# Pulling the conversion of a weight unit apart in the order of the work of a fused attention, gate and expert kernel

## The chip, the cores and the metric

The kernel runs on one core of a Trainium2 chip. The metric is the device time of one execution in microseconds (us), lower being better. Engines are called by the profile's names: PE is TensorE (PEld its weight loads), DVE is VectorE, ACT is ScalarE, POOL is GpSimd, and SP is SyncE, which here only issues transfers.

## The reference

Three stages follow one another, all in float32. The first is a gated linear recurrence over 768 steps for 4 x 8 heads of width 48, the second a gated feed-forward layer with 1536 hidden features, the third a choice of one of eight experts per token, each with 1024 hidden features.

```python
# stage 1, per batch and head
S_re, S_im = ar * S_re - ai * S_im + kv, ar * S_im + ai * S_re
y[:, :, t] = np.einsum('bhd,bhde->bhe', q[:, :, t], S_re)
...
# stage 2, 3072 tokens x 384; w_gate, w_val: 384 x 1536, w_out: 1536 x 384
xn = x / np.sqrt(np.mean(x * x, axis=-1, keepdims=True) + 1e-06) * rms_g
g = xn @ w_gate
x = (g / (1 + np.exp(-g)) * (xn @ w_val)) @ w_out
...
# stage 3
logits = xnorm @ en.T / tau          # en: 8 normalised expert embeddings
expert_idx = np.argmax(logits, axis=1)
out[mask] = gate_w[mask, None] * (np.maximum(x[mask] @ w1[e], 0.0) @ w2[e])
```

The three weights of stage 2 come in as float64, so each element has a low and a high 32-bit word.

## The kernel before, in words

The 3072 tokens are 24 tiles of 128. Stage 1 treats a tile in steps `s1` to `s10`; stage 2 treats blocks of two or three tiles (`BLOCKS`), and for each block runs over `NF` = 12 groups of 128 hidden features: `moe_g` (nine matmuls into `pg`, then a tanh on ACT and L799 on DVE), `moe_v` (nine matmuls into `pv`, L805, then the high part `hth` on ACT and the low part `htl` on DVE) and `moe_out` (three matmuls for each tile into `po`). While stage 2 works on one block, stage 1 prepares the tiles of the next.

Every float32 product is made of three matmuls with a high and a low part of each operand (`split_mm`). The parts of the weights are made once, during the first block, in 36 units: for each of the 12 groups one of w_gate, one of w_val, one of w_out. `conv_load(n)` lets SP load a unit (384 KB) into one of three `stg` buffers. `conv(n)` makes a float32 number out of the two words with three DVE instructions (L476 and L477 through the single buffer `ct`, L478 back into `raw`), copies it on ACT to the high part (L481), subtracts that on DVE for the low part (L482), and lets unit n + 3 be loaded.

For w_out there is also a fold. The router's logits come out of the same matmuls as the layer's output, in eight columns beside w_out's 384. For them PE turns the unit's `raw` by three transposes into a PSUM bank (`pwT`, L491), ACT copies it to SBUF (`wT`, L493), PE multiplies it by the embeddings in six passes (`pwe`, L496), and ACT and DVE make the two parts of the eight columns (L498, L499).

All steps are put on one list of events, each with a key in planned microseconds, and are written out in the order of the keys:

```python
for n in range(len(units)):
    at(CONV[0] + CONV[1] * n, conv, n)      # CONV = (-18.4, 1.85)
```

The first `moe_g` has key 0, and the first block has planned steps of 4.52 us for each group. Within what this order gives, the framework that compiles the kernel lays out each engine's instructions itself: of those that are ready by its own forecast, the one written first goes first. So the place of an instruction in the order is a priority, and the engines then work through their queues strictly in the order laid out.

Of the kernel before, what the change touches and what calls it, by code (L numbers as in the profile page):

```python
# [11 lines left out]
F32 = mybir.dt.float32  # L12
F32R = mybir.dt.float32r
I32 = mybir.dt.int32
AF = mybir.ActivationFunctionType
# [3 lines left out]
P = 128  # L19
# [14 lines left out]
T_BUFS = 3  # L34
# [66 lines left out]
SLOT = (0.0, 0.09, -0.43, 1.91, -1.0, -1.48, -0.61, -0.2, -0.3, -0.08, 0.0)  # L101
PACE = {0: 1.021, 2: 0.994}
CONV = (-18.4, 1.85)
ROUTE = 21.0
STARTUP = """
    s1.0 s1.1 s2.0 s2.1 s3a.0 s5a.0 s3a.1 s5a.1 s3b.0 s3b.1 s5b.0 s5b.1
# [185 lines left out]
def fused_kernel(ctx: ExitStack, tc: tile.TileContext, H, q, k, v, are, aim, wg, wv, wo, g, emb, tau, w1, w2, out):  # L292
    nc = tc.nc
    B, S, DM = q.shape
# [6 lines left out]
    NC = DM // P  # L301
# [30 lines left out]
    ident = beside[:, NC * E:]  # L332
# [31 lines left out]
    def bank(name):  # L364
        return psA.tile([P, 512], F32, tag="a", name=name)
# [90 lines left out]
    moe = wop.enter_context(tc.tile_pool(name="moe", bufs=1))  # L456
# [4 lines left out]
    units = [(src, dst, f) for f in range(NF) for src, dst in ((wg, WG), (wv, WV), (wo, WO))]  # L461
    raw_t = {}

    def conv_load(n):
        if n < len(units):
            src, _, f = units[n]
            raw_t[n] = moe.tile([P, DM, 2], I32, tag="stg", name="raw", bufs=STG_BUFS)
            nc.sync.dma_start(out=raw_t[n].rearrange("p x t -> p (x t)"), in_=src[f])

    def conv(n):  # L470

        _, dst, f = units[n]
        raw = raw_t.pop(n)
        lo, hi = raw[:, :, 0], raw[:, :, 1]
        t = moe.tile([P, DM], I32, tag="ct", name="ct", bufs=CT_BUFS)
        nc.vector.tensor_scalar(t, hi, 3, 0x3FFFFFF8, op0=ALU.logical_shift_left, op1=ALU.bitwise_and)  # L476
        nc.vector.scalar_tensor_tensor(out=t, in0=hi, scalar=-0x40000000, in1=t, op0=ALU.bitwise_and, op1=ALU.bitwise_or)  # L477
        nc.vector.scalar_tensor_tensor(out=hi, in0=lo, scalar=29, in1=t, op0=ALU.logical_shift_right, op1=ALU.bitwise_or)  # L478
        w = hi.bitcast(F32)
        dh, dl = (x[:, f, :DM] for x in dst)  # L480
        nc.scalar.activation(dh, w, AF.Copy)  # L481
        nc.vector.tensor_tensor(out=dl, in0=w, in1=dh.bitcast(F32), op=ALU.subtract)  # L482
        if dst is WO:
            fold(f, w)
        conv_load(n + 3)

    def fold(f, w):

        b = bank("pwT")
        for c in range(NC):  # L490
            nc.tensor.transpose(b[:, c * P:(c + 1) * P], w[:, c * P:(c + 1) * P], ident)  # L491
        wT = moe.tile([P, DM], F32, tag="t", name="wT", bufs=T_BUFS)
        nc.scalar.activation(wT, b[:, :DM], AF.Copy)  # L493
        pe = bank("pwe")[:, :E]
        for c in range(NC):
            nc.tensor.matmul(pe, wT[:, c * P:(c + 1) * P], enT[c], start=c == 0, stop=c == NC - 1)  # L496
        dh, dl = (x[:, f, DM:] for x in WO)
        nc.scalar.activation(dh, pe, AF.Copy)  # L498
        nc.vector.tensor_tensor(out=dl, in0=pe, in1=dh.bitcast(F32), op=ALU.subtract)  # L499
# [21 lines left out]
    st = {}  # L521
# [647 lines left out]
    def at(key, fn, *args):  # L1169
        events.append((key, len(events), fn, args))  # L1170
# [14 lines left out]
    for x, step in enumerate(STARTUP.split()):  # L1185
        fn, _, i = step.partition(".")
# [7 lines left out]
    at(-30.0, embed)  # L1194
    at(ROUTE, route_setup)
    start = 0.0
    prev = None
    for j, (t0, nt) in enumerate(blocks):
# [23 lines left out]
        if j:  # L1222
            jp, n = j - 1, blocks[j - 1][1]
# [8 lines left out]
            for x in range(per if j > 1 else 0):  # L1232
                n = (j - 2) * per + x
                at(start + (6.2 + 0.6 * x) * step, conv_load, n)
                at(start + (7.8 + 0.6 * x) * step, check_weight, n)
            for x in range(3 if j > 2 else 0):
                n = (j - 3) * 3 + x
# [3 lines left out]
        start += dur  # L1241
    for n in range(len(units)):
        at(CONV[0] + CONV[1] * n, conv, n)
    j = NB - 1
    t0, nt = blocks[j]
    begin = start - MOE_US * nt
# [85 lines left out]
```

## Time and profile before

| | |
|---|---|
| three runs | 1010.55, 1017.75, 1018.96 us; median 1017.75 us |
| profiled execution | 1016.29 us, of which the span of the trace 1014.5 us |
| busy share of the span | PE 94%, DVE 66%, ACT 60%, POOL 11% |
| mean granted clock of PE | 0.977 of full |

The span runs from the first to the last instruction; the remaining 1.8 us lie around it. A busy share is a mean over stages with different limits: the first block, in which the weights are converted, is only about an eighth of the span.

### The profile page before, as it was taken

Reading aid. Unit: us, or ns where it says so; the run is one execution under the profiler, and the core shown is the slowest. Engines: PE = TensorE matmul, PEld = TensorE weight load, DVE = VectorE, ACT = ScalarE, POOL = GpSimd, SP = SyncE. Lnnn points to the kernel's source line nnn. Section 1 sums busy time; section 2 is a strip of 40 time slices with the busy share of each in tenths; the row PEclk is TensorE's granted clock in tenths of the full one; section 3 lists DMA queues with packets and bytes.
Section 4 is the critical chain, followed back from the end, with each engine's and each line's share of the span. In section 5 each row is a group of like instructions: output and inputs, shape, how many; then the busy total and the mean of one; then the engine's idle time right before and its main releaser. Section 6 shows DMA issues by size and latency. Waiting matters only on the chain.

```text
span 1014.5 us, 19018 instructions
## 1 busy us (share of the span) xinstructions
PE 957.2 (94%) x7225; PEld 914.2 (90%) x7225; DVE 666.0 (66%) x1672; ACT 606.6 (60%) x1103; POOL 115.3 (11%) x174
## 2 busy tenths in 40 slices
PE   6968879999999999999999999999989999999995
PEld 5957778999999999999999999999988999999995
DVE  6887888777767867967976976654656544444420
ACT  7665757867678777767776855532434443455531
POOL 2000000100000100100010010010113211332211
PEclk9987789999999999999999999999999999999998
DMA  6353433215213412512511520300327423554200
GB/s 209 98 158 115 127 117 87 41 41 149 40 37 94 129 40 79 165 40 64 180 41 40 156 58 24 118 1 16 95 72 241 157 100 105 181 180 164 100 33 23
DMA packets 75539, 99.29 MB, mean 98 GB/s; under 512 B 27327, under 2 KB 57502, under 8 KB 75440
## 3 DMA queue, kind: packets, MB, share of 16 engines
q1 hardware_dynamic: 70272, 87.30, 28.9%
q0 software_dynamic: 5168, 10.70, 3.2%
q8 instruction: 58, 0.95, 0.4%
q14 instruction: 41, 0.34, 0.1%
HBM read 88.04 MB, written 10.50 MB: 97 GB/s over the span
## 4 chain that ended last, share of the span: by engine, by line
PE 73%; issue 8%; ACT 6%; DMA 5%; DVE 4%; POOL 1%; SPq 0%; POOLq 0%; ACTq 0%; DVEq 0%
PE pg L784 5%; PE po L784 4%; PE pg L785 4%; PE pg L786 4%; PE pv L784 4%; PE po L786 4%; PE pv L786 4%; PE pv L785 4%; PE po L785 4%; PE pAT L693 3%; PE ph L784 3%; PE ph L786 3%; PE ph L785 3%; PE eo L786 2%; PE eo L784 2%
## 5 line engine op out<-in xcount | busy, mean ns | idle before, releaser
L784 PE MATMUL pg<-xth,wg 128*128 128x384 f32 (+1 forms) x324 | 108.5, 335 | 7.8 <-DVE th L799 7.4
L436 ACT ACT_TABLE_LOAD x87 | 111.6, 1283 | 1.6
L784 PE MATMUL pv<-xth,wv 128*128 128x384 f32 (+1 forms) x324 | 106.7, 329 | 2.4 <-DVE th L805 2.4
L784 PE MATMUL po<-wo,hth 128*128 128x392 f32 x288 | 101.7, 353 | 3.6 <-ACT hth L807 3.6
L786 PE MATMUL pg<-xth,wg 128*128 128x384 f32 (+1 forms) x324 | 104.6, 323 | 0.0
L785 PE MATMUL pg<-xtl,wg 128*128 128x384 f32 (+1 forms) x324 | 104.5, 323 | 0.0
L786 PE MATMUL pv<-xth,wv 128*128 128x384 f32 (+1 forms) x324 | 104.4, 322 | 0.0
L785 PE MATMUL pv<-xtl,wv 128*128 128x384 f32 (+1 forms) x324 | 104.3, 322 | 0.0
L785 PE MATMUL po<-wo,hth 128*128 128x392 f32 x288 | 99.3, 345 | 0.0
L1083 DVE SCALAR_TENSOR_TENSOR hel<-ph,heh 128x256 fp32r<-128x256 f32 (+6 forms) x72 | 39.8, 553 | 89.9 <-ACT heh L1082 86.6
L786 PE MATMUL po<-wo,htl 128*128 128x392 f32 x288 | 98.5, 344 | 0.0
L436 ACT ACTIVATE th<-pg 128x384 f32<-128x384 f32 (+1 forms) x108 | 49.1, 455 | 80.1 <-PE pg L786 76.8
L807 ACT ACTIVATE hth<-th 128x384 fp32r<-128x384 f32 (+1 forms) x108 | 52.4, 485 | 67.2 <-DVE th L805 61.9
L1051 DVE TENSOR_TENSOR wl<-raw,wh 128x768 fp32r<-128x768 f32 x64 | 59.6, 955 | 33.7 <-ACT wh L1050 26.5
L1082 ACT ACTIVATE heh<-ph 128x256 fp32r<-128x256 f32 (+6 forms) x72 | 34.9, 485 | 75.4 <-PE ph L786 74.6
L799 DVE SCALAR_TENSOR_TENSOR th<-th,pg 128x384 f32<-128x384 f32 (+1 forms) x108 | 54.6, 506 | 33.7 <-ACT th L436 30.9
L784 PE MATMUL ph<-xeh,wh 128*128 128x256 f32 (+6 forms) x216 | 75.5, 350 | 0.0
L784 PEld LDWEIGHTS pg<-xth,wg 128*128 128x128 f32 x324 | 62.1, 192 | 12.8 <-DVE th L799 9.6
L786 PE MATMUL ph<-xeh,wl 128*128 128x256 f32 (+6 forms) x216 | 73.3, 339 | 0.0
L785 PE MATMUL ph<-xel,wh 128*128 128x256 f32 (+6 forms) x216 | 73.0, 338 | 0.0
L808 DVE TENSOR_TENSOR htl<-th,hth 128x384 fp32r<-128x384 f32 (+1 forms) x108 | 55.1, 511 | 22.3 <-ACT hth L807 20.7
L1050 ACT ACTIVATE wh<-raw 128x768 fp32r<-128x768 f32 x64 | 51.2, 839 | 29.6 <-DMA raw<-in_moe_w_dram 18.5
(250 smaller groups left out, 2500.5 us busy)
## 6 DMA issues: line engine op xcount, KB each, us to landing
raw<-in_moe_w_dram SPq DMA_DIRECT2D x32, 768.0 KB
raw<-in_moe_w_gate_dram SPq DMA_DIRECT2D x24, 384.0 KB
raw<-in_moe_w_val_dram SPq DMA_DIRECT2D x24, 384.0 KB
raw<-in_moe_w_out_dram SPq DMA_DIRECT2D x24, 384.0 KB
X<-in_a_im_dram SPq DMA_DIRECT2D x24, 192.0 KB
X<-in_a_re_dram SPq DMA_DIRECT2D x24, 192.0 KB
V<-in_v_dram SPq DMA_DIRECT2D x24, 192.0 KB
x2d<-row SPq DMA_DIRECT2D x24, 192.0 KB
```

The costliest lines, as they stand in the source:

```text
L436: chain[0] = fn(*args, **kw)
L693: nc.tensor.matmul(b[:, h * P:(h + 1) * P], KT[:D2, h], QT[:D2, h], start=True, stop=True)
L784: nc.tensor.matmul(o, lh, rh, start=start and x == 0, stop=False)
L785: nc.tensor.matmul(o, lh, rl, start=False, stop=False)
L786: nc.tensor.matmul(o, ll, rh, start=False, stop=stop and x == n - 1)
L799: nc.vector.scalar_tensor_tensor(out=t, in0=t, scalar=1.0, in1=b, op0=ALU.add, op1=ALU.mult)
L807: nc.scalar.activation(hh, t, AF.Copy)
L808: nc.vector.tensor_tensor(out=hl, in0=t, in1=hh.bitcast(F32), op=ALU.subtract)
L1050: nc.scalar.activation(dh, rw, AF.Copy)
L1051: nc.vector.tensor_tensor(out=dl, in0=rw, in1=dh.bitcast(F32), op=ALU.subtract)
L1082: nc.scalar.activation(hh, b, AF.Relu)
L1083: nc.vector.scalar_tensor_tensor(out=hl, in0=b, scalar=0.0, in1=hh.bitcast(F32), op0=ALU.max, op1=ALU.subtract)
```

## The change

The unit's work is spread over three events. `conv(n)` keeps the load's three DVE instructions and the copy to the high part. A new `split_weight(n)`, 1.2 units (2.22 planned us) later, makes the low part, for w_out also the transposes and the copy to `wT`, and lets unit n + 3 be loaded. `fold(f)`, 2.3 units (4.26 planned us) after the conversion, makes the eight columns. No instruction is added, removed or changed in size.

```diff
+SPLIT = (1.2, 2.3)
...
-        w = hi.bitcast(F32)
+        st["w", n] = hi.bitcast(F32)
+        nc.scalar.activation(dst[0][:, f, :DM], st["w", n], AF.Copy)
+
+    def split_weight(n):
+
+        _, dst, f = units[n]
+        w = st.pop(("w", n))
         dh, dl = (x[:, f, :DM] for x in dst)
-        nc.scalar.activation(dh, w, AF.Copy)
         nc.vector.tensor_tensor(out=dl, in0=w, in1=dh.bitcast(F32), op=ALU.subtract)
         if dst is WO:
-            fold(f, w)
+            b = bank("pwT")
+            for c in range(NC):
+                nc.tensor.transpose(b[:, c * P:(c + 1) * P], w[:, c * P:(c + 1) * P], ident)
+            st["wT", f] = moe.tile([P, DM], F32, tag="t", name="wT", bufs=T_BUFS)
+            nc.scalar.activation(st["wT", f], b[:, :DM], AF.Copy)
         conv_load(n + 3)
 
-    def fold(f, w):
-
-        b = bank("pwT")
-        for c in range(NC):
-            nc.tensor.transpose(b[:, c * P:(c + 1) * P], w[:, c * P:(c + 1) * P], ident)
-        wT = moe.tile([P, DM], F32, tag="t", name="wT", bufs=T_BUFS)
-        nc.scalar.activation(wT, b[:, :DM], AF.Copy)
+    def fold(f):
+
+        wT = st.pop(("wT", f))
         pe = bank("pwe")[:, :E]
...
     for n in range(len(units)):
         at(CONV[0] + CONV[1] * n, conv, n)
+        at(CONV[0] + CONV[1] * (n + SPLIT[0]), split_weight, n)
+        if n % 3 == 2:
+            at(CONV[0] + CONV[1] * (n + SPLIT[1]), fold, n // 3)
```

## Rows read from the trace of the kernel before

**Rows 1.** Busy time by stretch: its length, each engine's busy us, PE's clock, DMA.

```profile
46.00:166.00 120.00, 96.08 (x741) 87.04 (x741) 96.34 (x234) 73.36 (x143) 3.14 (x8) 0.86 0.40 119
...
200.00:1014.50 814.50, 791.95 (x5804) 763.54 (x5802) 503.72 (x1240) 471.94 (x850) 101.64 (x126) 0.99 0.31 93
```

**Rows 2.** DVE's waits, 46 to 180 us: us in total, times, longest.

```profile
DVE wo L499 <- ACT wo L498: 6.2, 8, 1.7
DVE wv L482 <- ACT wv L481: 3.3, 2, 2.3
DVE wg L482 <- ACT wg L481: 2.6, 2, 1.4
DVE ss L755 <- ACT XN L754: 2.3, 2, 1.9
...
DVE A L695 <- PE pAT L693: 1.4, 2, 0.9
DVE Sn L718 <- PE pKV L710: 0.6, 1, 0.6
```

**Rows 3.** PE's waits in the same stretch.

```profile
PE pwe L496 <- ACT wT L493: 6.2, 8, 2.0
PE pwT L491 <- issue: 5.8, 3, 2.7
```

**Rows 4.** ACT's longest group of waits in the same stretch.

```profile
ACT wo L481 <- DVE raw L478: 17.1, 7, 3.8
```

**Rows 5.** The transfer queue's longest group of waits, 0 to 180 us.

```profile
SPq L468 <- DVE wo L482: 23.1, 9, 4.2
```

**Rows 6.** Timeline of DVE around one unit of w_out, in order of time.

```profile
86.16 0.56 DVE L478 SCALAR_TENSOR_TENSOR raw<-raw,ct 128x384 int32<-128x384 int32 x1
...
87.63 0.55 DVE L482 TENSOR_TENSOR wo<-raw,wo 128x384 fp32r<-128x384 f32 x1
...
89.75 0.17 DVE L499 TENSOR_TENSOR wo<-pwe,wo 128x8 fp32r<-128x8 f32 x1 [1.01 <-ACT wo L498]
89.83 0.55 DVE L478 SCALAR_TENSOR_TENSOR raw<-raw,ct 128x384 int32<-128x384 int32 x1
...
96.51 0.15 DVE L755 TENSOR_SCALAR ss<-ss 128x1 f32<-128x1 f32 x1 [1.91 <-ACT XN L754]
```

**Rows 7.** Timeline of PE: the fold of that unit, and a later one.

```profile
86.82 0.60 PE L491 MATMUL pwT<-beside,raw 128*128 128x128 f32 x3 [1.83 <-issue]
88.06 1.45 PE L496 MATMUL pwe<-beside,wT 128*128 128x8 f32 x6 [0.64 <-ACT wT L493]
...
129.15 0.83 PE L496 MATMUL pwe<-beside,wT 128*128 128x8 f32 x6 [0.64 <-ACT wT L493]
```

**Rows 8.** Timeline of DVE: its four waits before a subtraction of wg or wv.

```profile
49.11 0.56 DVE L482 TENSOR_TENSOR wv<-raw,wv 128x384 fp32r<-128x384 f32 x1 [0.96 <-ACT wv L481]
...
78.88 0.56 DVE L482 TENSOR_TENSOR wg<-raw,wg 128x384 fp32r<-128x384 f32 x1 [1.41 <-ACT wg L481]
...
119.62 0.56 DVE L482 TENSOR_TENSOR wg<-raw,wg 128x384 fp32r<-128x384 f32 x1 [1.24 <-ACT wg L481]
...
151.18 0.56 DVE L482 TENSOR_TENSOR wv<-raw,wv 128x384 fp32r<-128x384 f32 x1 [2.33 <-ACT wv L481]
```

**Rows 9.** Groups that touch raw: shortest, median, longest ns; first and last start.

```profile
L476 DVE TENSOR_SCALAR ct<-raw x36: 338/353/450, 11.8 to 159.5; 128x384 int32<-128x384 int32 x36
...
L478 DVE SCALAR_TENSOR_TENSOR raw<-raw,ct x36: 536/553/560, 16.0 to 161.0; 128x384 int32<-128x384 int32 x36
...
L468 SPq DMA_DIRECT2D raw<-in_moe_w_gate_dram x12: 327/347/433, 6.0 to 146.4; - x12
...
L482 DVE TENSOR_TENSOR wg<-raw,wg x12: 528/550/560, 17.4 to 157.3; 128x384 fp32r<-128x384 f32 x12
```

**Rows 10.** Timelines of SP and DVE: the load with the shortest lead, and its use.

```profile
43.47 0.33 SPq L468 DMA_DIRECT2D raw<-in_moe_w_val_dram  x1
```

```profile
46.60 0.36 DVE L476 TENSOR_SCALAR ct<-raw 128x384 int32<-128x384 int32 x1 [0.21 <-DMA raw<-in_moe_w_val_dram]
```

## The prediction, made before the changed kernel was run

> **What bounds the kernel now.** I read the busy time by stretch first, because the mean over the span hides where this change lies. From 200 us on PE works 791.95 of 814.50 us at a clock of 0.99: that part is bound by PE, and nothing in it is touched. The first block, from 46 to 166 us, is another matter: PE is busy for 96.08 of 120 us at a clock of 0.86, DVE for 96.34, ACT for 73.36 [rows 1]. No engine is full there. DVE has the least to give: its work up to the end of the block is fixed, and PE's 96 us would shrink with a higher clock, while DVE's would not. So I take the block's end to be DVE's 96.34 us plus what DVE idles, 120 - 96.34 = 23.7 us. Later work on PE moves one for one with that end. The change can win at most 23.7 us, and only by taking DVE idle time away.
>
> Second, I read who waits for whom in that stretch. DVE waits longest before the last step of the fold, 6.2 us in 8 waits, and 3.3 + 2.6 = 5.9 us in four waits before the subtractions L482 of wv and wg; behind these come waits for stage 1 steps on PE and ACT, among them 2.3, 1.4 and 0.6 us [rows 2]. PE itself stands 6.2 us before the fold's six passes, because ACT has not yet copied `wT`, and 5.8 us before the transposes [rows 3]. That second wait is printed as "issue", but in the unit at 86 us the transposes start at 86.82, when L478 has just ended at 86.16 + 0.56 = 86.72 [rows 6, 7]: PE stands there for the converted numbers. ACT waits 17.1 us for the same L478 before copying w_out's high part [rows 4], and what stands behind that copy in its queue, a tanh among others, waits too.
>
> Third, the timeline of one fold. From L478's end at 86.72 to L499's start at 89.75 the chain over transposes, copy, six passes and L498 lasts 3.03 us, of which DVE idles the last 1.01 [rows 6, 7]. So the fold is a round trip through three engines, each of which works strictly in order.
>
> **The change part by part.** No instruction comes or goes, so all busy times stay; only places move. What moves is the priority in the order from which the engines' queues are laid out, so I price each part as if the instruction lands just behind the work that now outranks it.
>
> *Subtraction L482.* It now comes behind the next unit's three DVE instructions. Its four waits are 0.96, 1.41, 1.24 and 2.33 us [rows 8], together 5.94. A full-size DVE instruction of the conversion takes 0.55 us, the small L476 0.35 [rows 9]. At 78.88 two instructions of the next unit (L477, L478) still follow and can step in front: 1.1 us hidden. At 119.62 all three follow, 1.45 us: the whole 1.24 is hidden. At 151.18 only L478 follows: 0.55. At 49.11 the next unit isn't loaded yet: nothing. Sum 2.9 us gained; bounds 0 (the layout keeps its order) and 5.9.
>
> *Fold's end L499.* Its waits are 6.2 us. Of the 3.03 us chain, 88.06 - 86.72 = 1.34 us (transposes and copy) no longer stand directly ahead of the passes; the passes themselves, 0.83 us at the full clock and 1.45 at the lower one [rows 7], still stand directly ahead of L498 and L499. About half of the round trip leaves, so I take half: 3.1 us; bounds 0 and 6.2.
>
> *Transposes, copy and passes on PE and ACT.* PE's 12.0 us before them [rows 3] are not counted for themselves, as PE isn't the bound here. They count where DVE waits for what stands behind the fold in PE's queue: the longest of three groups, 1.9, 0.9 and 0.6 us [rows 2], follow a fold directly (the one at 96.51 goes back over PE to the fold at 88.06 [rows 6, 7]). Half of these 3.4 us is 1.7; bounds 0 and 3.4.
>
> *The load of unit n + 3.* This is the price. SP issues it once a buffer is free, and already waits 23.1 us, 9 times, for the L482 of a w_out unit [rows 5]. Nothing else on SP waits for it, save that the in-order queue can now put it behind a load of V or QK that itself waits. I set L482 of each unit behind the next unit's L478: over 35 pairs that is 2.6 us later on average (36 units, [rows 9]; in the unit at 87.63 it is 89.83 + 0.55 - 87.63 = 2.75 [rows 6]). Then I compare each of the 33 later loads with its use: the lead from issue to L476 runs from 3.13 to 10.4 us. At 3.13 DVE waited 0.21 us for the landing [rows 10], so 3.13 us is about what a load takes. Eleven loads would come late, by 14.0 us together. Three of them (units 6, 7 and 9, 10.8 us) lie between 36 and 54 us, where buffers are held by the first two transposes of w_out, and where a subtraction can't stay behind a unit that waits for its own buffer; I leave those out. The other eight make 3.2 us. Bounds 0 and 14.0.
>
> [...]
>
> *`wT` and the PSUM banks.* `wT` is held longer in a tag of three buffers, which it shares with `th`; one `th`, at times two, is alive, so I cost this at nothing. If two were always alive, a tanh would wait for the six passes, up to 1.45 us a time [rows 7].
>
> *Sum.* 2.9 + 3.1 + 1.7 - 3.2 = 4.5 us gained. The profiled execution took 1016.29 us (span 1014.5 and 1.8 around it), which gives 1011.8. It lies 1.46 us under the median of the three runs, so I forecast 1013. With all gains and no price it is 1017.75 - 15.5 = 1002; with the whole price and no gain 1032.
>
> **The rivals.** *The whole stretch tightens, PE's clock included: 1003.* [...] If the 12 us before the fold go and the clock comes back, transposes and scores of stage 1 reach DVE sooner, and the waits of rows 2 shrink by about 14 to 15 us. For it speaks that gaps precede the slow passages; against it, that PE's waits for `th` and `hth` come from DVE and stay. [...]
>
> *Nothing moves: 1017.* The order is only a priority: where an engine is free in the forecast of the layout, it takes the transposes as soon as they are ready, whatever their key. PE has room, so the fold may stay where it is.
>
> *Late loads bind: slower, 1029.* With a buffer held 2.6 us longer in each of 36 units, all eleven late loads hold up DVE: 14.0 us, less the 2.9 at L482, on 1017.75. It decides from the point where the lead of the loads after 50 us, mostly 5 to 6 us now, falls under 3.13. Against it: DVE lays out other work in front where the load isn't there.
>
> **How the numbers follow.** The forecast (1008 to 1017 for itself) has 0.47, the tight stretch 0.22, no movement 0.17, late loads 0.14. The three runs before spread over 8.4 us, so a change within 1% (10.2 us) can hardly be told from none. Faster by over 1%, under 1007.6: the tight stretch and the low edge of the forecast, 0.27. Slower by over 1%, above 1027.9: most of the late loads, 0.11. Within: 0.62. The range from 1002 to 1025 leaves out most of the late loads and a low tail, under 0.2 together.
>
> **What would show it.** In the profile after: L482 of a unit behind the next unit's L478 on DVE, its waits near 3 us; the passes `pwe` no longer waiting for `wT`; L499's waits near 3; the first block ending some 5 us sooner, and the work after it unchanged in length. I am wrong if L476 shows waits for loads of several us, if ACT's wait before w_out's copy grows, or if the first block ends early and the gain is given back later.

## The result: 1.3% faster, and the profile after

The changed kernel took 1000.78 us in the median of four runs (999.60 to 1003.51), the kernel before 1016.23 us in its four (1010.55 to 1018.96): a ratio of 0.9868, 95% interval 0.9826 to 0.9909. The interval lies wholly below 1: a small gain, but clear of the spread, and about three times what the forecast's sum gave. The profiled execution took 1003.51 us, with a span of 1001.8 us, 12.7 us less than before.

In the changed file L477 to L479 are the three instructions of the conversion, L488 is the subtraction, L492 the transposes, L494 the copy to `wT`, L502 the six passes, and L504 and L505 make the eight columns.

First, where in the span the time was won. These are the busy times by stretch of the kernel after, the two that answer to [rows 1] and then the stretch from 46 us to the start of the last subtraction (length, PE, PEld, DVE, ACT and POOL busy, PE's clock, DMA):

```profile
46.00:166.00 120.00, 103.17 (x865) 92.40 (x864) 106.16 (x276) 85.81 (x172) 4.13 (x11) 0.93 0.45 131
200.00:1001.80 801.80, 778.91 (x5697) 749.83 (x5687) 495.85 (x1225) 462.50 (x833) 102.13 (x125) 0.99 0.31 93
...
46.00:150.30 104.30, 87.65 (x748) 77.27 (x747) 92.47 (x230) 73.60 (x144) 3.26 (x9) 0.92 0.48 142
```

The stretch up to the last subtraction in the kernel before:

```profile
46.00:162.30 116.30, 92.96 (x681) 84.79 (x679) 94.18 (x230) 71.35 (x138) 3.14 (x8) 0.85 0.41 123
```

The last subtraction comes after 104.3 instead of 116.3 us. DVE does 230 instructions in both; its busy time goes from 94.2 to 92.5, its idle time from 22.1 to 11.8 us. So 10.3 of the 12.0 us are DVE idle time taken away, and PE's clock rises from 0.85 to 0.92. The same 12.0 us can be booked on PE: 5.3 us less busy time, though with 748 instead of 681 instructions, and 6.7 us less idle time. The split by DVE alone doesn't tell which engine carried the gain. The groups of the first stage 2 result rows, of before and after (x24: shortest, median, longest ns, then first and last start):

```profile
L828 ACT ACTIVATE row<-po x24: 473/492/508, 172.1 to 753.1; 128x384 f32<-128x384 f32 x24
```

```profile
L834 ACT ACTIVATE row<-po x24: 474/492/504, 157.3 to 739.5; 128x384 f32<-128x384 f32 x24
```

The first block ends 14.8 us sooner, and 13.6 of that is still there at the end of stage 2: what lies behind is bound by PE and only shifts.

Second, the waits. DVE's in the kernel after, 46 to 150.3 us (total, times, longest):

```profile
DVE wg L488 <- ACT wg L481: 4.1, 3, 3.3
DVE wo L505 <- ACT wo L504: 1.7, 1, 1.7
DVE ct L477 <- DMA raw<-in_moe_w_gate_dram: 1.3, 2, 0.7
DVE xtl L783 <- ACT xth L782: 1.2, 1, 1.2
DVE QK L631 <- ACT En L437: 1.2, 1, 1.2
DVE wv L488 <- ACT wv L481: 0.9, 1, 0.9
DVE htl L814 <- ACT hth L813: 0.8, 1, 0.8
DVE A L701 <- PE pAT L699: 0.4, 1, 0.4
DVE ct L477 <- DMA raw<-in_moe_w_val_dram: 0.3, 1, 0.3
DVE th L805 <- ACT th L437: 0.2, 1, 0.2
```

In the kernel before, 46 to 162.3 us, beside the lines of [rows 2] for wv, wg, A and Sn, which hold for this stretch too:

```profile
DVE wo L499 <- ACT wo L498: 5.5, 7, 1.7
DVE ss L755 <- ACT XN L754: 1.9, 1, 1.9
DVE xtl L777 <- ACT xth L776: 1.9, 2, 1.2
DVE R L635 <- ACT R L634: 1.7, 1, 1.7
DVE th L799 <- ACT th L436: 1.2, 2, 0.9
DVE htl L808 <- ACT hth L807: 1.1, 1, 1.1
```

I sort these lines by whose work is waited for. Before the subtraction: 5.9 us before, 5.0 after. Before the eight columns: 5.5, now 1.7. For a load: 0.2, now 1.6. For steps of stage 1 and of the hidden features (ss, xtl, R, A, th, htl, Sn, QK): 1.9 + 1.9 + 1.7 + 1.4 + 1.2 + 1.1 + 0.6 = 9.8, now 3.8. The last sort fell most, though none of these steps was touched.

Third, the same unit of w_out as in [rows 6, 7], in PE's timeline after:

```profile
83.65 0.52 PE L492 MATMUL pwT<-beside,raw 128*128 128x128 f32 x3
...
84.25 0.81 PE L607 MATMUL T<-X,triS 128*128 128x384 f32 x2
84.89 0.89 PE L607 MATMUL L<-X,triS 128*128 128x384 f32 x2
...
86.69 0.28 PE L792 MATMUL pv<-xth,wv 128*128 128x256 f32 x1
86.84 0.83 PE L502 MATMUL pwe<-beside,wT 128*128 128x8 f32 x6
```

and in DVE's:

```profile
81.65 0.55 DVE L479 SCALAR_TENSOR_TENSOR raw<-raw,ct 128x384 int32<-128x384 int32 x1
...
84.59 0.14 DVE L761 TENSOR_SCALAR ss<-ss 128x1 f32<-128x1 f32 x1
...
90.87 0.16 DVE L505 TENSOR_TENSOR wo<-pwe,wo 128x8 fp32r<-128x8 f32 x1
```

The transposes start 1.45 us after L479 has ended (82.20) and wait for nothing; the passes start 3.2 us after them, with other matmuls between, `T` and `L` of stage 1 among them; the passes run at the faster pace (0.83, not 1.45 us) amid `pv`; the columns' low part follows 3.2 us after their end without a wait. And `ss`, for which DVE stood 1.91 us in [rows 6], is there when DVE comes to it.

That wait for `ss` shows a second thing. PE makes `pKV` and eight groups `pyT` for it: before, right behind the fold of [rows 7]; after, ahead of the same unit's fold. First and last of them, before with the clock, then after:

```profile
89.44 1.50 PE L710 MATMUL pKV<-V,KF 128*32 128x48 f32 x48
...
93.91 0.54 PE L740 MATMUL pyT<-QT,Sn 96*64 96x128 f32 x4
```

```profile
88.00:92.00 4.00, 3.94 (x66) 3.80 (x68) 2.24 (x7) 2.80 (x7) 0.77 (x1) 0.50 0.35 103
```

```profile
79.61 0.88 PE L716 MATMUL pKV<-V,KF 128*32 128x48 f32 x48
...
82.01 0.39 PE L746 MATMUL pyT<-QT,Sn 96*64 96x128 f32 x4
```

Before, PE had stood 1.83 and 0.64 us at the fold [rows 7], its clock was then 0.50, and this work took 5.01 us; after, it takes 2.79 us at a clock of 1.00. The difference of 2.2 us is more than the 1.91 us that DVE waited. So this wait can be owed to the clock as much as to the place in the queue.

### The profile page after: what moved, and what is told of

Read it like the earlier page. It is cut to its first block, busy times and chain, and to the rows that moved or that the text cites. A ratio compares the mean times of both kernels' runs of the same rounds, so it can differ in the third digit from the quotient of the medians.

```text
span 1001.8 us, 19020 instructions
## 1 busy us (share of the span) xinstructions
PE 951.2 (95%) x7225; PEld 905.6 (90%) x7225; DVE 663.4 (66%) x1672; ACT 605.5 (60%) x1103; POOL 116.0 (12%) x174
## 4 chain that ended last, share of the span: by engine, by line
PE 69%; DVE 9%; issue 8%; DMA 6%; ACT 5%; POOL 1%; SPq 0%; POOLq 0%; ACTq 0%; DVEq 0%
PE pg L790 4%; PE pv L790 4%; PE po L790 4%; PE pg L791 4%; PE pg L792 4%; PE pv L791 4%; PE po L792 4%; PE pv L792 4%; PE po L791 4%; PE pAT L699 3%; PE ph L790 3%; PE ph L791 3%; PE ph L792 3%; PE eo L791 2%; PE eo L792 2%
## 5 line engine op out<-in xcount | busy, mean ns | idle before, releaser
L791 PE MATMUL pv<-xtl,wv 128*128 128x384 f32 (+1 forms) x324 | 104.3, 322 | 0.0
L1089 DVE SCALAR_TENSOR_TENSOR hel<-ph,heh 128x256 fp32r<-128x256 f32 (+6 forms) x72 | 39.9, 554 | 90.5 <-ACT heh L1088 87.7
```

What stands on the lines that cost most here:

```text
L791: nc.tensor.matmul(o, lh, rl, start=False, stop=False)
L1089: nc.vector.scalar_tensor_tensor(out=hl, in0=b, scalar=0.0, in1=hh.bitcast(F32), op0=ALU.max, op1=ALU.subtract)
```

## The experiments

Each ratio is to the kernel before, run beside it on the same chip; a 95% interval stands in brackets. Where nothing else is said, a shown line of busy times is the stretch from 46 us to the last subtraction's start. DVE's idle time is the length less its busy time. The lines come from one execution of each run, which need not be a typical one: that of sub_late (1014.09 us) and that of fill_low (1026.66) were the slowest of ten, that of half (1011.78) the slowest but one, and that of sub_early (998.90) the fastest of four.

**Only the eight columns late** (fold_late).

```diff
-        at(CONV[0] + CONV[1] * (n + SPLIT[0]), split_weight, n)
+        at(CONV[0] + CONV[1] * n, split_weight, n)
```

> Only the eight columns (six passes, L498, L499 of before) are put 2.3 units later; the low part, the transposes, the copy to wT and the load stay with the conversion. If the gain is the fold's round trip taken apart, this alone gives most of it: 1001 to 1006 us, no waits of PE for wT, and the columns' wait on DVE under 2.5 us. If the lower place of the subtraction and the transposes does it, this stays at 1012 to 1017. If any change of the order that closes PE's gaps helps through the clock, the time follows the clock of the first block: 0.92 and about 1002, or 0.86 and about 1016.

Ratio 0.9924 [0.9898, 0.9950], 1007.08 us. Busy times by stretch, and PE's longest waits in it:

```profile
46.00:153.20 107.20, 84.30 (x671) 77.06 (x670) 93.56 (x227) 70.49 (x138) 3.27 (x8) 0.90 0.45 133
```

```profile
PE pwT L492 <- issue: 5.5, 2, 3.7
PE pg L790 <- DVE th L805: 4.9, 2, 2.8
...
PE pwT L492 <- DVE raw L479: 3.0, 2, 2.1
```

Over half of the gain, a little short of what I expected. PE waits for `wT` only once more, for 0.6 us, but it waits longer for the converted numbers, 8.5 us before the transposes. DVE's idle time is down to 13.6 us all the same. The third theory fits too: between its two points (0.86 and 1016 us, 0.92 and 1002) the clock of 0.90 asks for about 1007 us.

**The fold late as a whole** (split_late).

```diff
-SPLIT = (1.2, 2.3)
+SPLIT = (1.2, 1.2)
```

> Low part, transposes, copy, load and the eight columns all come 1.2 units after the conversion, the eight columns straight behind the transposes. The fold is as closely knit as before, only later as a whole. Round trip theory: little gained, 1010 to 1016, PE still waits 4 us or more for wT. Theory that the lower priority of all this work is what counts (conversion and tanh go first): 1001 to 1006.

Ratio 0.9916 [0.9874, 0.9958], 1006.07 us:

```profile
46.00:153.20 107.20, 86.86 (x741) 76.67 (x739) 92.67 (x230) 73.85 (x144) 3.37 (x9) 0.92 0.47 137
```

My theory of the round trip missed here: a fold as closely knit as before, but 1.2 units later, gains as much as the columns alone, and DVE idles 14.5 us. Lower priority counts, not only the distance between the links; the clock is 0.92 here as well. DVE still waits 4.2 us before the columns in this run.

**Only the subtraction and the load late** (sub_late).

```diff
     def conv(n):
...
+        # transposes and copy to wT, as in split_weight
     def split_weight(n):
...
         nc.vector.tensor_tensor(out=dl, in0=w, in1=dh.bitcast(F32), op=ALU.subtract)
         conv_load(n + 3)
...
-            at(CONV[0] + CONV[1] * (n + SPLIT[1]), fold, n // 3)
+            at(CONV[0] + CONV[1] * n, fold, n // 3)
```

> Only the subtraction for the low part and the load come 1.2 units later; transposes, copy and eight columns stay with the conversion. The predicted 2.9 us at the subtraction less 3.2 us for late loads: 1016, within 3 us of before. If the subtraction's place were the cause of the gain: 1001 to 1008.

Ratio 0.9968 [0.9943, 0.9993], 1011.62 us:

```profile
46.00:161.20 115.20, 94.73 (x676) 85.10 (x675) 93.31 (x227) 71.49 (x139) 3.14 (x8) 0.82 0.41 124
```

A small gain, with DVE's idle time unchanged at 21.9 us in the execution shown. Its waits before the subtraction are 3.0 us there instead of 5.9, the 2.9 us that I had set, but waits at other lines (A 4.0, th 3.7) make up for them. In its timeline the subtraction stands behind the next unit's last conversion instruction in 6 of 35 units (1 before, 7 in the changed kernel): the lower priority hardly moves it. I take it that the layout found it ready before its rivals; no run shows that.

**All but the subtraction late** (sub_early).

```diff
     def conv(n):
...
+        nc.vector.tensor_tensor(out=dl, in0=w, in1=dh.bitcast(F32), op=ALU.subtract)
     def split_weight(n):
...
-        nc.vector.tensor_tensor(out=dl, in0=w, in1=dh.bitcast(F32), op=ALU.subtract)
```

> As the changed kernel, but the subtraction stays with the conversion; transposes, copy and load come 1.2 units later, the eight columns 2.3 units later. If the fold is the cause: as the changed kernel, 999 to 1004. If the subtraction carries 2.9 us of the gain: 1003 to 1006.

Ratio 0.9885 [0.9834, 0.9935], 1001.37 us, as the changed kernel (0.9868):

```profile
46.00:150.20 104.20, 85.74 (x745) 75.38 (x744) 92.93 (x228) 73.81 (x144) 3.43 (x9) 0.93 0.48 141
```

The subtraction's place adds nothing that can be seen; the intervals, half a per cent to either side, would hide its 2.9 us. The transposes, the copy, the load and the columns carry the gain, and since early_load below gains nothing by earlier loads, the fold's later place is the cause.

**Only the columns' two halves late, the passes in place** (cols_late). The passes' result goes to SBUF by an added copy.

```diff
+        st["pc", f] = sm.tile([P, E], F32, tag="pc", name="pc")
+        nc.scalar.activation(st["pc", f], pe, AF.Copy)
...
+        pc = st.pop(("pc", f))
-        nc.scalar.activation(dh, pe, AF.Copy)
-        nc.vector.tensor_tensor(out=dl, in0=pe, in1=dh.bitcast(F32), op=ALU.subtract)
+        nc.scalar.activation(dh, pc, AF.Copy)
+        nc.vector.tensor_tensor(out=dl, in0=pc, in1=dh.bitcast(F32), op=ALU.subtract)
```

> As the kernel before, but ACT first copies the six passes' result to a small SBUF tile (12 added copies of 128x8), and only the two halves of the eight columns (L498, L499 of before) are made 2.3 units later; the transposes, the copy to wT and the passes stay with the conversion. If DVE's own wait before L499 (5.5 us) is what the later fold saves: 1009 to 1011 us and no such wait. If the passes standing in PE's queue ahead of stage 1 work are the cause: no gain, 1013 to 1017.

Ratio 0.9983 [0.9959, 1.0007], 1012.17 us. Busy times, then DVE's longest waits:

```profile
46.00:159.80 113.80, 90.72 (x681) 81.55 (x679) 94.28 (x230) 72.84 (x149) 3.14 (x8) 0.87 0.43 126
```

```profile
DVE wg L488 <- ACT wg L481: 4.3, 4, 2.7
DVE A L707 <- PE pAT L705: 3.6, 3, 2.4
...
DVE wo L511 <- ACT wo L510: 2.6, 3, 1.7
```

DVE's wait before the columns falls from 5.5 to 2.6 us, and the time is the same within the interval: other waits (wg 4.3 for 2.6, A 3.6 for 1.4) take its place. What DVE waits for is late anyhow, as PE still does the passes early and ACT waits 4.6 us for them in the added copy (4.2 us before, at L498). The 12 copies are also 2.1 us of added work on ACT, so this run takes that one wait away and not the whole fold's end.

**PE kept busy** (filled: 48 groups of six 128x128 matmuls of `ones` and `ident` in planned order, float32; fill_low: 12 groups of 16 in float32r, the type of the split weights, of the lowest priority in the block).

```diff
+    def fill(n):
+        b = psO.tile([P, 512], F32, tag="o2", name="fill")
+        for _ in range(n):
+            nc.tensor.matmul(b[:, :P], ones, ident, start=True, stop=True)
...
+    for n in range(48):
+        at(0.3 + 1.1 * n, fill, 6)
```

```diff
+        w = WG[0][:, f, :P]
+        for _ in range(16):
+            nc.tensor.matmul(b[:, :P], w, w, start=True, stop=True)
...
+    for n in range(NF):
+        at(53.5, fill, n)
```

> The kernel before with 288 matmuls of 128x128 that nobody reads, written into a PSUM bank that is free in the first block, spread over that block. They keep PE busy without changing what waits for what. If the clock of PE is what the change gave back: clock of the first block from 0.85 to 0.95 and more, and 1001 to 1008 us. If the waits come from the order of the queues: clock up, time 1012 to 1022.

> The kernel before with 192 short matmuls that nobody reads (high-part weights, 128x128, about 0.06 us each), 16 for each feature group, of the lowest priority in the first block, into a free PSUM bank: about 12 us of PE work in gaps of 23 us, where the 576 longer ones of the run named filled had made PE full. If PE's clock is the cause of the gain: clock of the first block over 0.90 and 1005 to 1011 us. If the cause is what stands in the queues ahead of stage 1 work: clock up, time 1012 to 1019.

filled: ratio 1.0245 [1.0202, 1.0288], 1038.12 us. fill_low: 1.0028 [1.0000, 1.0056], 1020.87 us. Their stretches, and the group of the added instructions in the first (288 matmuls appear as 576):

```profile
46.00:153.30 107.30, 107.01 (x977) 102.19 (x976) 90.48 (x215) 63.72 (x124) 3.22 (x8) 1.00 0.45 134
```

```profile
L389 PE MATMUL fill<-beside,ones x576: 269/275/378, 50.3 to 191.7; 128*128 128x128 f32 x192
```

```profile
46.00:155.80 109.80, 100.99 (x805) 94.12 (x803) 94.35 (x229) 71.51 (x140) 3.15 (x8) 0.91 0.43 131
...
L835 ACT ACTIVATE row<-po x24: 473/492/505, 180.6 to 760.0; 128x384 f32<-128x384 f32 x24
```

The first made PE full and tells only that PE's time in this block isn't free. The second brings the clock from 0.85 to 0.91, near the 0.92 of the changed kernel, and the last subtraction comes 6.5 us sooner: DVE's idle time is 15.5 instead of 22.1 us, although 122 of the added matmuls take 18.5 us of PE there (0.15 us each, not the 0.06 that I had expected; a third of the 0.17 us from start to start of the 128x384 matmuls at 230 to 236 us of the kernel before would be 0.06). But the first block's rows come at 180.6, 8.5 us later than before. The other 70 added matmuls lie in between. From the last subtraction to the first row, of fill_low and of before:

```profile
155.80:180.60 24.80, 23.65 (x192) 21.91 (x191) 9.29 (x25) 7.39 (x17) 0.22 (x2) 0.72 0.10 25
```

```profile
162.30:172.10 9.80, 8.60 (x119) 7.48 (x119) 7.15 (x21) 7.20 (x16) 0.22 (x2) 1.00 0.26 62
```

The added matmuls take 13.6 us of PE there, and the clock is 0.72 instead of 1.00. So the run as a whole is no faster, and yet it doesn't speak against the clock: in the stretch where the clock rose, DVE's idle time fell with no step moved on purpose. What the clock is worth by itself this run doesn't measure.

**Half of the distances** (half, from sub_early).

```diff
-SPLIT = (1.2, 2.3)
+SPLIT = (0.6, 1.15)
```

> As the run sub_early, but transposes 0.6 and eight columns 1.15 units later, half of 1.2 and 2.3. Round trip theory: between before and sub_early, 1003 to 1010, since half of the distance between the links is there. If it only matters that conversion and other steps of equal key go first: as sub_early, 999 to 1003.

Ratio 0.9925 [0.9893, 0.9956], 1010.36 us:

```profile
46.00:157.80 111.80, 91.32 (x676) 82.63 (x675) 93.32 (x228) 71.33 (x139) 3.21 (x8) 0.85 0.43 128
```

0.75% are gained in the median. The execution shown took 1011.78 us, 0.55% under the median before, at a clock of 0.85 in this stretch, that of the kernel before; its groups `pyT` up to 140 us still take 421 ns a matmul in the median, as against 272 in the changed kernel. So a part of the gain comes without any help of the clock.

**More distance for the columns** (later).

```diff
-SPLIT = (1.2, 2.3)
+SPLIT = (1.2, 4.0)
```

> As the changed kernel, but the eight columns 4.0 instead of 2.3 units later. Round trip theory: the trip is already open at 2.3, so the same time within 3 us, 998 to 1004; if each unit of delay buys more: 993 to 998.

Ratio 0.9922 [0.9888, 0.9957], 1005.34 us. No more was gained; whether a part is lost again, the intervals don't tell.

**A new order without a purpose** (jitter, from the kernel before).

```diff
-CONV = (-18.4, 1.85)
+CONV = (-18.0, 1.85)
```

> The kernel before with all conversions 0.4 planned us later: a change of the order without a purpose. If the gain is owed to the fold being pulled apart: 1012 to 1019. If nearly any new order of the first block is better than the one before: under 1010.

Ratio 1.0022 [0.9996, 1.0048], 1016.33 us: this one arbitrary shift of the conversion gains nothing.

**Loads as early as can be** (early_load, from sub_early).

```diff
     def conv(n):
...
+        if dst is not WO:
+            conv_load(n + 3)
     def split_weight(n):
...
-        conv_load(n + 3)
+            conv_load(n + 3)
```

> As the run sub_early, but a unit of w_gate or w_val lets the next load go straight after its subtraction; only the units of w_out load after their transposes. If later loads cost the 3.2 us of the prediction: 997 to 999. If loads are hidden anyway: 1000 to 1003, and waits of DVE for loads under 1 us.

Ratio 0.9903 [0.9875, 0.9931], 1007.13 us. DVE's waits for loads in it:

```profile
DVE ct L477 <- DMA raw<-in_moe_w_val_dram: 1.7, 1, 1.7
...
DVE ct L477 <- DMA raw<-in_moe_w_out_dram: 1.2, 1, 1.2
```

No gain, and 2.9 us of waits for loads, more than the 0.8 of sub_early and the 1.6 of the changed kernel. Later loads didn't cost the 3.2 us that I had set for them.

**The changed kernel once more** (after_again).

> The changed kernel itself once more, beside the three others on the same chip: 999 to 1004.

Ratio 0.9868 [0.9810, 0.9925], 1002.48 us. No run was clearly faster than the changed kernel; sub_early can't be told from it, with one step less moved.

## Why the prediction was right, and where its sum fell short

The direction and the place were right, the size was not: 4.5 us were forecast and some 15 came. The time lies 1.2 us under the low end of the range; taken as a ratio to the 1017.75 us from which the forecast started it would be 1004.3, just inside. The forecast gave 0.62 to a change within 1% and 0.27 to what came. And that the two terms which failed at the subtraction and at the load (2.9 and -3.2) nearly cancel in the sum is luck.

*The place.* That the first block alone is concerned, and that later work only shifts, held. That the block's end is DVE's work plus DVE's idle time is true by the way it is counted, and the gain shows there: DVE's idle time up to the last subtraction fell by 10.3 us, the end by 12.0, and 13.6 of the 14.8 us at the end of the first block were still there at the end of stage 2.

*Subtraction, 2.9 us.* Wrong for the changed kernel. Its waits are 5.0 instead of 5.9 us, and 5.1 in sub_early, which leaves it in place and gains as much within the intervals. I had set it behind the next unit's instructions; the layout did that in 7 of 35 units. That is the rival "nothing moves", and for this instruction it was nearly right. In sub_late its waits did fall by 2.9 us, and the time by 0.3%.

*Fold's end, 3.1 us.* The wait shrank by 3.8 us, near the estimate, but taken away by itself it is worth little: cols_late took away 2.9 us of it and gained 0.17%, with an interval that holds zero.

*Transposes, copy and passes on PE and ACT, 1.7 us.* This is the term that was mis-sized. I counted the three groups of waits that directly follow a fold and took half. DVE's waits for all steps of stage 1 and of the hidden features fell from 9.8 to 3.8 us, 6.0. My account is that everything in the queues of PE and ACT stood behind the fold, twelve times over, and that each delay reached DVE at another line. ACT's wait for L478 (now L479) before w_out's copy, which was to grow if I was wrong, fell from 17.1 to 8.1 us. fold_late (two links parted) and split_late (the whole fold behind other work) each gain about 0.8%, together 1.3%: two ways to let the other steps pass, which seem to overlap. The 6.0 us are measured; that the queues alone gave them isn't shown, as the `ss` of the section on the result tells.

*Load, -3.2 us.* Too dear. DVE waits 1.6 us for loads where it waited 0.2, so the price was at most 1.4 us, and the earlier loads of early_load bought nothing. I had moved each load by the full 2.6 us of a subtraction that mostly stayed in place. The slow rival fell with that: SP waits even longer for subtractions than before (39.9 us for 34.9, 0 to 180 us), and the kernel is faster.

*The sum.* As measured: 0.9 at the subtraction, 3.8 at the columns, 6.0 at the other steps, less 1.4 for loads, gives 9.3 us of the 10.3 us of idle time; the other 1.7 us of the 12.0 are less DVE busy time in the stretch, at the same 230 instructions. What makes up this difference I have not traced.

*The tight stretch, 1003 us.* The time came out near this rival, and the clock rose to 0.92. Its 14 to 15 us at the waits were my estimate; measured are 10.3 us less DVE idle time. PE's gaps and clock aren't the whole of the gain: half gains while the clock stays at 0.85, and cols_late, whose `pyT` groups up to 140 us take 272 ns a matmul in the median, gains nothing that can be told from zero. But they can be much of it. The `ss` wait and the first stretch of fill_low speak for that. So does the kernel before by itself: its 23 executions beside half run from 1022.97 us at a mean clock of 0.969 over the span to 1010.44 at 0.981. A straight line through them gives 0.85 us for each 0.001. On average half is 7.8 us faster than they are, and 4.0 us faster than the line at its own clock; after_again is 14.8 us faster than they are, and 6.2 us faster than the line. Which of the two draws the other along, the line doesn't tell. So the fold's later place is the cause, and how its gain divides between queues that are free sooner and a clock that is less often low stays open, as no run changes the clock alone. In windows of 1 us from 46 to 162 us of the kernel before, the clock is 1.00 in 77, 0.50 in 28 and between the two in 11; from 46 to 150 us of the changed kernel it is so in 85, 13 and 6. Why the layout gives a little less at 4.0 than at 2.3 units is open too.

## What to carry to other kernels

Price a chain that goes through three engines with strict queues (in the kernel before, DVE's 1.91 us wait for `ss` also held up the next unit's L476 right behind it, 8.35 us after the issue of its load) by all that stands behind its links, not by the waits printed at its own lines: here its own waits were 5.5 us on DVE, and DVE's waits at other steps shrank by 6.0 us. Look at PE's clock behind such a chain as well, since it can be part of what the chain costs: here the 5.01 us at a clock of 0.52 that were 2.79 at 1.00. Where a scheduler lays out the queues, a lower priority can leave a step where it was, as here 28 of 35 subtractions; look in the trace for who could pass before counting on it. And take a wait away by itself before calling it a term of the sum: one that only marks how late its producer is can come back at another line. Read a run with added work stretch by stretch, because its total also holds what the added work costs.

## What the runs showed of the hardware that I had not expected

PE's time was not free in a stretch in which it idled 23 us: in fill_low's execution, the slowest of its ten, the first block ended 8.5 us later, although the clock rose from 0.85 to 0.91 up to the last subtraction. After that subtraction PE was busy for 23.65 of 24.80 us at a clock of 0.72. And 288 float32 matmuls of 128x128 were 576 instructions on PE, which is why the first filling was far too large.
